# Seven block products instead of eight for the first f pair of a token pair's output, and two places for weights

## Chip, cores and metric

The kernel runs on one core of a Trainium2 chip. The metric is the device time in microseconds (us), the median of the runs; lower is better.

## What is computed

The reference is a channel attention and a mixture layer without routing behind it, over 4 batches of 6080 tokens with 256 channels and 2048 hidden features, all in float32:

```python
qn = q / (norm(q, axis=1) + 1e-06)          # q, k, v: (4, 6080, 256)
kn = k / (norm(k, axis=1) + 1e-06)
a = softmax(kn.transpose(0, 2, 1) @ qn / tau)   # (4, 256, 256)
x = (v @ a).reshape(24320, 256)
h = x @ w_in                                # w_in: (256, 2048)
g = where(h >= 1, h, where(h <= -1, 0, (h + 1) ** 2 / 4))
return g @ w_out                            # w_out: (2048, 256)
```

The attention's matrix is small, so the kernel multiplies it into w_in once per batch: the weights of a batch are a @ w_in, and h is v times these weights.

## The kernel before

**Precision.** A float32 value is held as two parts, a high one rounded for TensorE and a low one, the rest. `mm3` (L470 to L474) makes a product of two such values by three matmuls: high by high, high by low, low by high. Each matmul loads its 128x128 weights anew.

**Tiles and groups.** A batch has six token pairs: two tiles of 512 tokens each, of 480 in the last pair. The 2048 features are eight f pairs: two tiles of 128 features each. A group is one f pair of one token pair: 4 x 6 x 8 = 192 groups, f pairs innermost (`groups`). In one group h is a 2x2 block product (256 channels by 256 features, times two token tiles), and `strassen` (L640 to L656) makes it by 7 products of blocks: S1, S2, S3, S4 and A11, A12, A22 are sums or blocks of the weights, T1 to T4 and V11, V21, V22 those of v. Three PSUM banks carry them: A, B and one of two Z. In bank Z four of them run one after another, and between them ACT copies the bank (L644, L646) and DVE adds to it (L649, L653).

**The nonlinearity.** `tile_ops` (L782 to L799) makes g of each of the four h tiles of a group: ACT saturates (L790) and squares (L792), DVE takes the maximum with h (L794), ACT or DVE makes the high part (L796, L797), DVE the low part (L798). The pools are u (6 places of 512 columns) and g (7 places of two parts of 512).

**The output.** `o_ops` (L820 to L844) multiplies the four tiles by blocks of w_out, 8 products a group, two for each of the four output blocks (y, the token tile; ct, the channel tile). Each output block has a bank of its own, O00 to O11, in which it sums over the eight groups of a token pair; then ACT copies it (L838) and SP stores it to outT.

**Weights.** Each group needs 896 KB of weights in a place of pool w (w_mem, 4 places). In the first token pair of a batch they are computed or taken from what was computed (`make_W`, `take_W`; POOL makes the sums at L702, ACT the high parts at L706, DVE the low parts) and stored to w_d; in all others `load_W` reads them back from w_d.

**Work for the next batch** runs beside the groups: `gram_chunk` (k and q products), `square_piece` (squares of norms), `softmax` (which sends norms through HBM as rn_d and the matrix as e_d), `make_W7` (weights), and `make_V` for the next token pair (POOL subtractions at L746).

**What sets the order.** Every instruction is an `Op` with an engine, a modelled duration, what it reads and writes, and a due time; group g begins at due time 16 g. `Order.run` simulates the engines and hands out instructions one by one: on each engine the one that can start earliest, among those that can start now the one with the lowest due time. A place of a pool is free when all users of its last holder have been handed out, from the modelled end of the last of them. The program then runs in this order, each engine strictly in its own; SP issues every DMA.

Of the kernel before, what the change touches and what calls it, by code (L numbers as in the profile page):

```python
# [13 lines left out]
ALU = mybir.AluOpType  # L14
# [12 lines left out]
class Buf:  # L27


    def __init__(self, pool=None, ap=None):  # L30
        self.pool, self.ap = pool, ap
# [19 lines left out]
SOON = 0.3  # L51

# [6 lines left out]
class Order:  # L59
# [11 lines left out]
    def op(self, eng, dur, fn, r=(), w=(), due=0.0, gates=(), size=0, other=None, slack=0.0):  # L71
# [20 lines left out]
        o.bufs = list({id(b): b for b in (*r, *w)}.values())  # L92
# [32 lines left out]
    def run(self):  # L125
# [23 lines left out]
        while left:  # L149
            pick = None  # L150
            for e, ops in avail.items():
                now = free[e]
                best = None
                for o in ops:
                    t = base[o.n, e]
                    if best is not None and t > now + SOON and t >= best[0][0]:
                        continue
# [11 lines left out]
                    key = (now, o.due, o.n) if t <= now or o.due <= URGENT and t <= now + SOON else (t, o.due, o.n)  # L169
# [10 lines left out]
            for b in o.bufs:  # L180
                if b.ap is None:
# [4 lines left out]
                    b.ap = b.pool.aps[i]() if callable(b.pool.aps[i]) else b.pool.aps[i]  # L186
            for b in o.bufs:
# [38 lines left out]
U = 32  # L226
# [17 lines left out]
ET_SLACK = (2.0, 3.0)  # L244

# [10 lines left out]
def channel_attention_moe(ctx: ExitStack, tc: tile.TileContext, kq, kqT, vT, tau, w_in, w_out, outT):  # L256
# [42 lines left out]
    wout = sb("wout", [FP, 2, 2, C], F32R)  # L299

# [4 lines left out]
    def slot2(j, h):  # L305
# [3 lines left out]
        return late[j][:, h]  # L309

    w_mem = sb("w_mem", [4 * 2 * NS * P], F32R)
# [5 lines left out]
    u_mem = sb("u_mem", [6 * TB])  # L317
# [7 lines left out]
        "g": Pool([sb("g6", [2, TB], F32R), *[lambda j=j, h=h: slot2(j, h) for j in range(3) for h in range(2)]]),  # L325
        "w": Pool([w_mem[:, i * WSZ:(i + 1) * WSZ].rearrange("p (a j f) -> p a j f", a=2, j=NS) for i in range(4)]),
# [4 lines left out]
        "u": Pool([u_mem[:, i * TB:(i + 1) * TB] for i in range(6)]),  # L331
# [21 lines left out]
    pools["g"].held[1:] = [kq_all] * 6  # L353
# [10 lines left out]
    pools["u"].held[:4] = [u2_all] * 4  # L364
# [10 lines left out]
    def buf(pool):  # L375
        return Buf(pools[pool])
# [6 lines left out]
    def convert(src, out, dst, due, gates=(), step=0.4, load_due=None, n=1, keep=None):  # L383
# [6 lines left out]
        cb = buf("u" + two)  # L390
# [16 lines left out]
        if keep is not None:  # L407
# [4 lines left out]
           r=[cb, *out], w=out, due=due + 4 * step)  # L412

    wout_buf = [Buf(ap=wout[:, i]) for i in range(FP)]
    x_store = [Buf(ap=d) for d in x_dram]
# [5 lines left out]
    def make_w_out(i, due, gates=(), load_due=None):  # L421

        convert(w_out[i:i + 2].rearrange("n p a f -> p n (a f)"), wout_buf[i:i + 2],
                lambda x: wout[:, i:i + 2, x].rearrange("p n a f -> p n (a f)"), due, gates, load_due=load_due, n=2)
# [567 lines left out]
```

## Time and profile before

| | us |
|---|---|
| median of 3 runs | 2160.39 (2159.62 to 2161.54) |
| span of the profiled execution | 2158.3 |
| PE busy | 2147.2 |
| DVE busy | 1783.1 |
| ACT busy | 1593.0 |
| POOL busy | 245.0 |

The span is one execution's time from its first to its last instruction; the median is taken from whole runs and has some 2 us around it. Busy time is the time in which an engine works on something: PE is TensorE, DVE is VectorE, POOL is GpSimd, SP issues the DMAs. A busy time near the span tells which engine to look at first; whether it works without gaps, the waits and the stages tell.

### The profile page before, as it was taken

The numbers are of one execution on the slowest core, as the hardware profiler recorded it, in microseconds if no ns is written. First come the engines' busy times: TensorE is split into PE (matmuls) and PEld (weight loads), VectorE is DVE, ScalarE is ACT, GpSimd is POOL, SyncE is SP. The second block draws the span as 40 slices with busy tenths as digits, with TensorE's granted clock in tenths as the row PEclk, the third lists the DMA queues.
The fourth block names the chain that finished last, engine by engine and source line by source line (L and its number), as shares of the span: only waits on it lengthen the run. The fifth ranks groups of instructions, "written<-read, shape, count | busy, mean of one in ns | idle before, by whom it ended". The sixth has DMA issues, their size and how long they took to land.

```text
span 2158.3 us, 27952 instructions
## 1 busy us (share of the span) xinstructions
PE 2147.2 (99%) x9872; PEld 1802.1 (83%) x9872; DVE 1783.1 (83%) x2893; ACT 1593.0 (74%) x2818; POOL 245.0 (11%) x260
## 2 busy tenths in 40 slices
PE   9999999999999999999999999999999999999999
PEld 7888888888888888888888888888888888888887
DVE  7898888878798888888879888888787988777776
ACT  6687778777778777776778877777677777777776
POOL 0230020100131000000023000000012300001000
PEclk9999999999999999999999999999999999999999
DMA  9765366545665444544656455454556532332331
GB/s 385 299 225 172 130 205 206 174 164 156 202 222 181 172 158 163 202 156 133 198 174 234 173 183 172 154 192 140 138 201 202 173 124 91 132 126 94 121 120 36
DMA packets 124604, 371.46 MB, mean 172 GB/s; under 512 B 17968, under 2 KB 49584, under 8 KB 121904
## 3 DMA queue, kind: packets, MB, share of 16 engines
q1 hardware_dynamic: 124464, 369.67, 50.1%
q8 instruction: 78, 1.28, 0.2%
q14 instruction: 62, 0.51, 0.1%
HBM read 298.84 MB, written 70.78 MB: 171 GB/s over the span
## 4 chain that ended last, share of the span: by engine, by line
PE 96%; DMA 2%; DVE 1%; ACT 0%; POOL 0%; issue 0%; SPq 0%; ACTq 0%; DVEq 0%; POOLq 0%
PE bank L473 94%; PE bank L875 1%; DMA kq<-kq 1%; DMA raw_mem<-w_out 1%; DMA raw_mem<-vT 0%; DMA outT<-y_mem 0%; DVE mh_mem L891 0%; POOL t L746 0%; DVE u_mem L404 0%; ACT u_mem L790 0%; DVE w_mem L708 0%; ACT u_mem L792 0%; POOL cols L532 0%; DVE v L755 0%; DVE u_mem L401 0%
## 5 line engine op out<-in xcount | busy, mean ns | idle before, releaser
L473 PE MATMUL bank<-x,wout 128*128 128x512 f32 (+1 forms) x3948 | 1013.4, 388 | 0.0
L473 PEld LDWEIGHTS bank<-x,wout 128*128 128x128 f32 x3948 | 739.3, 188 | 147.0
L473 PE MATMUL bank<-v,w_mem 128*128 128x512 f32 (+1 forms) x3264 | 849.3, 388 | 1.1 <-ACT bank L646 0.6
L473 PEld LDWEIGHTS bank<-v,w_mem 128*128 128x128 f32 x3264 | 610.8, 188 | 122.9 <-ACT bank L646 1.2
L790 ACT ACTIVATE u_mem<-bank 128x512 f32<-128x512 f32 (+1 forms) x576 | 341.3, 593 | 252.9 <-PE bank L473 240.4
L794 DVE TENSOR_TENSOR u_mem<-bank,u_mem 128x512 f32<-128x512 f32 (+1 forms) x576 | 390.9, 680 | 131.3 <-ACT u_mem L792 130.2
L792 ACT ACTIVATE u_mem<-u_mem 128x512 f32<-128x512 f32 (+1 forms) x768 | 471.0, 626 | 6.8
L798 DVE TENSOR_TENSOR x<-u_mem,x 128x512 fp32r<-128x512 f32 (+1 forms) x658 | 457.1, 701 | 13.8 <-ACT x L796 8.7
L796 ACT CAST x<-u_mem 128x512 fp32r<-128x512 f32 (+1 forms) x300 | 183.9, 615 | 92.7 <-DVE u_mem L794 91.6
L649 DVE TENSOR_TENSOR bank<-bank,mh_mem 128x512 f32<-128x512 f32 (+1 forms) x198 | 137.2, 693 | 96.8 <-PE bank L473 93.0
L473 PE MATMUL bank<-x,w_mem 128*128 128x512 f32 (+1 forms) x768 | 208.8, 388 | 0.9 <-ACT bank L646 0.9
L473 PE MATMUL bank<-g,wout 128*128 128x512 f32 (+1 forms) x660 | 182.8, 387 | 0.0
L746 POOL TENSOR_TENSOR t<-raw_mem 128x512 f32<-128x512 f32 (+1 forms) x48 | 67.8, 1411 | 925.0 <-DMA raw_mem<-vT 542.7
L653 DVE TENSOR_TENSOR mh_mem<-bank,mh_mem 128x512 f32<-128x512 f32 (+1 forms) x198 | 135.6, 685 | 40.2 <-PE bank L473 35.2
L473 PEld LDWEIGHTS bank<-x,w_mem 128*128 128x128 f32 x768 | 143.6, 188 | 30.0 <-ACT bank L646 1.3
L797 DVE CAST x<-u_mem 128x512 fp32r<-128x512 f32 (+1 forms) x358 | 159.6, 452 | 8.0
L644 ACT COPY mh_mem<-bank 128x512 f32<-128x512 f32 (+1 forms) x198 | 115.3, 582 | 59.4 <-PE bank L473 57.3
L794 DVE TENSOR_TENSOR u_mem<-mh_mem,u_mem 128x512 f32<-128x512 f32 (+1 forms) x192 | 135.6, 706 | 13.6 <-ACT u_mem L792 13.3
L473 PEld LDWEIGHTS bank<-g,wout 128*128 128x128 f32 x660 | 123.7, 188 | 24.5
L646 ACT COPY bank<-bank 128x512 f32<-128x512 f32 (+1 forms) x198 | 113.4, 573 | 33.7 <-PE bank L473 28.0
L746 POOL TENSOR_TENSOR t<-raw_mem,t 128x512 f32<-128x512 f32 (+1 forms) x48 | 66.8, 1392 | 496.3 <-DVE v L755 394.1
L790 ACT ACTIVATE u_mem<-mh_mem 128x512 f32<-128x512 f32 (+1 forms) x192 | 118.9, 619 | 5.1 <-DVE mh_mem L653 3.7
(104 smaller groups left out, 1432.5 us busy)
## 6 DMA issues: line engine op xcount, KB each, us to landing
w_mem<-w_d SPq DMA_DIRECT2D x160, 896.0 KB, 4.6
raw_mem<-kqT SPq DMA_DIRECT2D x60, 512.0 KB, 6.2
w_d<-w_mem SPq DMA_DIRECT2D x32, 896.0 KB, 4.5
raw_mem<-kq SPq DMA_DIRECT2D x51, 512.0 KB, 5.5
kq<-kq SPq DMA_DIRECT2D x20, 1024.0 KB, 9.1
raw_mem<-vT SPq DMA_DIRECT2D x40, 512.0 KB, 6.3
outT<-y_mem SPq DMA_DIRECT2D x80, 256.0 KB, 2.8
win_mem<-wop_d SPq DMA_DIRECT2D x21, 512.0 KB, 5.6
```

The costliest lines, as they stand in the source:

```text
L473: nc.tensor.matmul(out, lhsT=lhs(a), rhs=rhs(c), start=start and m == 0, stop=stop and m == 2, skip_group_check=skip)
L644: op("ACT", act_us(n), lambda: nc.scalar.copy(m5.ap[:, :n], a.ap[:, :n]), r=[a], w=[m5], due=early)
L646: op("ACT", act_us(n), lambda: nc.scalar.copy(a.ap[:, :n], z.ap[:, :n]), r=[z], w=[a], due=early)
L649: op("DVE", dve_us(n), lambda: nc.vector.tensor_tensor(out=bb.ap[:, :n], in0=z.ap[:, :n], in1=m5.ap[:, :n], op=ALU.add), r=[z, m5], w=[bb] ...
L653: op("DVE", dve_us(n), lambda: nc.vector.tensor_tensor(out=h22.ap[:, :n], in0=z.ap[:, :n], in1=m5.ap[:, :n], op=ALU.add), r=[z, m5], w=[h2 ...
L746: op("POOL", pool_us(n), lambda: nc.gpsimd.tensor_tensor(out=tt(x), in0=a(), in1=c(), op=ALU.subtract), r=r, w=[ts[x]], due=due + d, gates ...
L790: op("ACT", act_us(n), lambda: nc.scalar.activation(us(), src(), IDENTITY_SAT240, scale=240.0), r=[h], w=[u], due=d_sat)
L792: op("ACT", act_us(n), lambda: nc.scalar.activation(us(), us(), AF.Square, bias=0.5, scale=1.0 / 480.0), w=[u], due=d_sq)
L794: op("DVE", dve_us(n), lambda: nc.vector.tensor_tensor(out=us(), in0=src(), in1=us(), op=ALU.max), r=[h], w=[u], due=d_max)
L796: op("ACT", act_us(n), lambda: nc.scalar.copy(t.ap[:, 0, :n], us()), r=[u], w=[t], due=d_hi, other=("DVE", dve1_us(n), lambda: nc.vector.t ...
L797: other=("DVE", dve1_us(n), lambda: nc.vector.tensor_copy(t.ap[:, 0, :n], us())) if g >= FIRST else None)
L798: op("DVE", dve_us(n), lambda: nc.vector.tensor_tensor(out=t.ap[:, 1, :n], in0=us(), in1=f32(t.ap[:, 0, :n]), op=ALU.subtract), r=[u], w=[ ...
```

## The change

The first f pair (i = 0) of every token pair but a batch's first (SPLIT) makes its output blocks by 7 products instead of 8. Four go straight to the four output banks (`direct`): two with blocks of w_out, two with sums of blocks (`wsum`, made once from w_out by DVE and ACT). Then the bank O01 goes on alone: ACT keeps a copy of it, a fifth product is added, DVE keeps the sum of it and a copy of O11, a sixth product is added, ACT keeps a copy, a seventh is added. The three kept tiles are added by DVE to the other three blocks when these are stored, in place of the ACT copy; O01 is then already whole. POOL makes the four differences of g tiles that the seven products need (`combos`), and three of these differences get high and low parts of their own.

To make room, pool w has two places instead of four. Pool u has 5 places of 1024 columns (one for two tiles), g has 4 places of two tiles; c and c2 hold the differences and the kept tiles. Due times are written out anew for groups of both kinds (T_PLAIN, T_STR; the numbers of T_PLAIN and most of T_STR are left out below), and a few others move. Operations on g tiles, in `tile_ops` before, are in `sat_ops`, `square_ops`, `max_ops` and `operand`, with the same instructions. The planner gets a branch for operations that start within AHEAD.

```diff
+AHEAD, RATE = -21.03, 40.8
...
-                    if best is not None and t > now + SOON and t >= best[0][0]:
+                    if best is not None and t > now + max(SOON, AHEAD) and t >= best[0][0]:
...
+                    if t <= now or o.due <= URGENT and t <= now + SOON:
+                        key = (now, o.due, o.n)
+                    elif t <= now + AHEAD and e in ("ACT", "DVE"):
+                        key = (now, o.due + RATE * (t - now), o.n)
+                    else:
+                        key = (t, o.due, o.n)
...
-U = 32
+U = 32.76
...
+SPLIT = ((0, 1, 1, 1, 1, 1), (0, 1, 1, 1, 1, 1), (0, 1, 1, 1, 1, 1), (0, 1, 1, 1, 1, 1))
+WN = 2
...
+T_STR = {
...
+    'sum': (30.04, 31.22, 27.0, 22.88),
+    'direct': (21.09, 27.49, 26.88, 27.74),
+    'chain': (30.85, 43.19, 53.35),
...
+    wsum = sb("wsum", [max(map(max, SPLIT)), 2, 4, P], F32R)
...
-    w_mem = sb("w_mem", [4 * 2 * NS * P], F32R)
+        return late[j] if h is None else late[j][:, h]
+
+    w_mem = sb("w_mem", [WN * 2 * NS * P], F32R)
...
-        "g": Pool([sb("g6", [2, TB], F32R), *[lambda j=j, h=h: slot2(j, h) for j in range(3) for h in range(2)]]),
-        "w": Pool([w_mem[:, i * WSZ:(i + 1) * WSZ].rearrange("p (a j f) -> p a j f", a=2, j=NS) for i in range(4)]),
+        "g": Pool([*[sb(f"g{i}", [2, 2, TB], F32R) for i in range(1)], *[lambda j=j: slot2(j) for j in range(3)]]),
+        "w": Pool([w_mem[:, i * WSZ:(i + 1) * WSZ].rearrange("p (a j f) -> p a j f", a=2, j=NS) for i in range(WN)], ordered=True),
...
-        "u": Pool([u_mem[:, i * TB:(i + 1) * TB] for i in range(6)]),
+        "u": Pool([u_mem[:, i * 1024:(i + 1) * 1024] for i in range(5)]),
+        "c": Pool([sb(f"c{i}", [TB]) for i in range(4)]),
+        "c2": Pool([sb(f"cc{i}", [2, TB]) for i in range(1)]),
...
+    def sum_w_out(k, part, cb, due):
+        t, o = buf("u", TB), wsum_buf[k]
+        tt = lambda m: t.ap[:, m * P:(m + 1) * P]
+        for m, a, c, o_ in ((0, lambda: part(0, 1), lambda: part(1, 1), ALU.add),
+                            (1, lambda: tt(0), lambda: part(0, 0), ALU.subtract),
+                            (2, lambda: part(0, 0), lambda: part(0, 1), ALU.subtract),
+                            (3, lambda: part(1, 0), lambda: tt(1), ALU.subtract)):
+            op("DVE", dve_us(P), lambda m=m, a=a, c=c, o_=o_: nc.vector.tensor_tensor(out=tt(m), in0=a(), in1=c(), op=o_),
+               r=[cb], w=[t], due=due)
+        flat = lambda a: wsum[:, k, a].rearrange("p m f -> p (m f)")
+        op("ACT", act_us(TB), lambda: nc.scalar.copy(flat(0), t.ap), r=[t], w=[o], due=due + 1)
+        op("DVE", dve_us(TB), lambda: nc.vector.tensor_tensor(out=flat(1), in0=t.ap, in1=f32(flat(0)), op=ALU.subtract),
+           r=[t], w=[o], due=due + 2)
...
+        u0, u1 = gu[g] = pair(), pair()
+        q = T_STR if i < SPLIT[b][k] else T_PLAIN
...
+        if i < SPLIT[b][k]:
+            combos(g)
+        at = lambda k: [(x, d + e) for x, e in q[k]]
+        gt[g, 1] = operand(u1, n, (at("hi1"), at("lo1")))
+        gt[g, 0] = operand(u0, n, (at("hi0"), at("lo0")))
...
+    def combos(g):
+        b, k, i = groups[g]
...
+        c2, c = sums[b, k, i] = buf("c2"), buf("c")
+        c2.parts, c.parts = [Buf(ap=()), Buf(ap=())], [Buf(ap=())]
+        for k_, out, o, a, x, c_, y in ((0, c2, 1, u1, 1, u1, 0), (1, u1, 0, u1, 0, u0, 0), (2, c2, 0, u1, 1, u1, 0),
+                                        (3, c, 0, u0, 1, c2, 0)):
+            op("POOL", pool_us(n), lambda out=out, o=o, a=a, x=x, c_=c_, y=y: nc.gpsimd.tensor_tensor(
+                out=half_of(out, o, n), in0=half_of(a, x, n), in1=half_of(c_, y, n), op=ALU.subtract),
+               r=[a.parts[x], c_.parts[y]], w=[out.parts[o]], h=[out, a, c_], due=d + T_STR["sum"][k_])
...
+    def strassen_o(g):
...
+        w_ = lambda j, x, ct: (lambda a: wout[:, j, a, x, ct * P:(ct + 1) * P])
+        s_ = lambda j, m: (lambda a: wsum[:, j, a, m])
...
+        first = T_STR["direct"]
+        mm(o(0, 1), w_(i, 0, 0), wout_buf[i], gt[g, 0], 0, i == 0, d + first[0])
+        mm(o(1, 0), s_(i, 3), wsum_buf[i], gt[g, 1], 1, i == 0, d + first[1])
+        mm(o(1, 1), s_(i, 0), wsum_buf[i], gt[g, 1], 0, i == 0, d + first[2])
+        mm(o(0, 0), w_(i, 1, 0), wout_buf[i], gt[g, 0], 1, i == 0, d + first[3])
+        if i < SPLIT[b][k] - 1:
+            return
+        r = sums[b, k] = {x: buf("c") for x in ((0, 0), "m5", (1, 0), (1, 1))}
+        early = d + T_STR["early"]
+        z = o(0, 1)
+
+        def copy(src, x):
+            op("ACT", act_us(n), lambda: nc.scalar.copy(r[x].ap[:, :n], src.ap[:, :n]), r=[src], w=[r[x]], due=early)
+
+        copy(z, (0, 0))
+        copy(o(1, 1), "m5")
+        late = lambda key, j: [(x, d + e + T_STR["late"] * (j - i)) for x, e in T_STR[key]]
+        t23 = [operand(sums[b, k, j][0], n, (late("hi2", j), late("lo2", j))) for j in range(SPLIT[b][k])]
+        for j in range(SPLIT[b][k]):
+            mm(z, s_(j, 1), wsum_buf[j], t23[j], 0, False, d + T_STR["chain"][0])
+        op("DVE", dve_us(n), lambda: nc.vector.tensor_tensor(out=r[1, 0].ap[:, :n], in0=z.ap[:, :n], in1=r["m5"].ap[:, :n],
+                                                            op=ALU.add), r=[z, r["m5"]], w=[r[1, 0]], due=early)
+        for j in range(SPLIT[b][k]):
+            mm(z, s_(j, 2), wsum_buf[j], t23[j], 1, False, d + T_STR["chain"][1])
+        copy(z, (1, 1))
+        for j in range(SPLIT[b][k]):
+            t = operand(sums[b, k, j][1], n, (late("hi4", j), late("lo4", j)))
+            mm(z, w_(j, 1, 1), wout_buf[j], t, 0, False, d + T_STR["chain"][2])
...
+                    r = sums.get((b, k), {}).get((y, ct))
+                    if r:
+                        op("DVE", dve_us(n), lambda o=o, yb=yb, r=r: nc.vector.tensor_tensor(
+                           out=yb.ap[:, :n], in0=o.ap[:, :n], in1=r.ap[:, :n], op=ALU.add), r=[o, r], w=[yb], due=due)
+                    else:
+                        op("ACT", act_us(n), lambda o=o, yb=yb: nc.scalar.copy(yb.ap[:, :n], o.ap[:, :n]), r=[o], w=[yb],
+                           due=due)
...
-            make_V(*groups[g + 4][:2], d + 8, gate(g), 7.0)
+            make_V(*groups[g + 4][:2], d + 8.3, gate(g), 5.42)
...
-                softmax(b + 1, d + 8)
+                softmax(b + 1, d + 19.26)
...
-    nc = bacc.Bacc("TRN2", target_bir_lowering=False, num_devices=1)
+    nc = bacc.Bacc("TRN2", target_bir_lowering=False, num_devices=1, dynamic_dma_scratch_size=1024)
```

## Rows read from the trace of the kernel before

**Rows 1.** The page: span; part 1, busy time by engine; part 4, the chain.

```profile
span 2158.3 us, 27952 instructions
...
PE 2147.2 (99%) x9872; PEld 1802.1 (83%) x9872; DVE 1783.1 (83%) x2893; ACT 1593.0 (74%) x2818; POOL 245.0 (11%) x260
...
PE 96%; DMA 2%; DVE 1%; ACT 0%; POOL 0%; issue 0%; SPq 0%; ACTq 0%; DVEq 0%; POOLq 0%
```

**Rows 2.** Waits of PE: waiter, released by: total us, times, longest us (first, last).

```profile
PE bank L875 <- DMA kq<-kq: 3.0, 4, 1.7
...
PE bank L473 <- DVE u_mem L794: 0.2, 1, 0.2
```

**Rows 3.** Stages: length, busy us (instructions) by engine, PE's clock, DMA share, GB/s.

```profile
100.00:150.00 50.00, 49.81 (x242) 41.86 (x241) 48.81 (x74) 40.07 (x74) 16.26 (x19) 1.00 0.60 211
1150.00:1250.00 100.00, 100.00 (x475) 84.01 (x474) 88.69 (x137) 79.08 (x138) 15.09 (x18) 1.00 0.58 202
1850.00:1950.00 100.00, 100.00 (x443) 82.84 (x442) 76.92 (x128) 71.16 (x127) 8.37 (x6) 1.00 0.36 123
```

**Rows 4.** Timeline of PE in batch 3: start, us, engine, line, operation, count.

```profile
1753.88 2.88 PE L473 MATMUL bank<-x,wout 128*128 128x512 f32 x12
1756.60 1.52 PE L473 MATMUL bank<-v,w_mem 128*128 128x512 f32 x6
```

**Rows 5.** Groups by line and form: busy us, mean ns | idle before, released by.

```profile
L798 DVE TENSOR_TENSOR x<-u_mem,x 128x512 fp32r<-128x512 f32 x549 | 385.2, 709 | 11.7 <-ACT x L796 7.6
...
L796 ACT CAST x<-u_mem 128x512 fp32r<-128x512 f32 x255 | 157.3, 619 | 69.7 <-DVE u_mem L794 68.5
...
L797 DVE CAST x<-u_mem 128x512 fp32r<-128x512 f32 x294 | 131.9, 455 | 6.4
...
L644 ACT COPY mh_mem<-bank 128x512 f32<-128x512 f32 x166 | 97.4, 587 | 54.9 <-PE bank L473 52.9
...
L746 POOL TENSOR_TENSOR t<-raw_mem,t 128x512 f32<-128x512 f32 x40 | 56.6, 1416 | 419.6 <-DVE v L755 334.7 <-DVE x L755 83.3
...
L838 ACT COPY y_mem<-bank 128x512 f32<-128x512 f32 x80 | 46.7, 583 | 14.2 <-PE bank L473 6.7 <-DMA outT<-y_mem 6.4
```

**Rows 6.** Timeline of PE in batch 3: S1, the last product before, next S1.

```profile
1781.76 0.84 PE L473 MATMUL bank<-v,w_mem 128*128 128x512 f32 x3
1782.44 0.84 PE L473 MATMUL bank<-x,w_mem 128*128 128x512 f32 x3
...
1791.96 0.84 PE L473 MATMUL bank<-v,w_mem 128*128 128x512 f32 x3
```

**Rows 7.** Timeline of ACT in batch 0, and at 1020 in batch 1.

```profile
119.87 0.59 ACT L644 COPY mh_mem<-bank 128x512 f32<-128x512 f32 x1 [0.67 <-PE bank L473]
...
121.92 0.94 ACT L706 CAST w_mem<-sf_mem 128x896 fp32r<-128x896 f32 x1
...
1020.79 0.59 ACT L644 COPY mh_mem<-bank 128x512 f32<-128x512 f32 x1 [0.40 <-PE bank L473]
```

**Rows 8.** Timeline of POOL, then of DVE, in batch 3.

```profile
1783.19 1.38 POOL L746 TENSOR_TENSOR t<-raw_mem,t 128x512 f32<-128x512 f32 x1
...
1783.79 1.33 DVE L794 TENSOR_TENSOR u_mem<-mh_mem,u_mem 128x512 f32<-128x512 f32 x1 [0.36 <-ACT u_mem L792]
...
1785.98 0.68 DVE L794 TENSOR_TENSOR u_mem<-bank,u_mem 128x512 f32<-128x512 f32 x1
```

**Rows 9.** DMA into w_mem: issues; SP's timeline; landing from 1010 and 1545.

```profile
w_mem<-w_d SPq DMA_DIRECT2D x160, 896.0 KB, 4.6
...
1019.81 0.37 SPq L556 DMA_DIRECT2D rn_d<-cols  x1
1021.47 0.32 SPq L379 DMA_DIRECT2D w_mem<-w_d  x1
...
DMA to landing us min/median/max: 13.5/13.5/13.5
...
DMA to landing us min/median/max: 12.6/12.6/12.6
```

More of the change, by code (lines that the diff above doesn't have):

```diff
@@ L69, in __init__, with op @@
         self.ops = []
-    def op(self, eng, dur, fn, r=(), w=(), due=0.0, gates=(), size=0, other=None, slack=0.0):
+    def op(self, eng, dur, fn, r=(), w=(), due=0.0, gates=(), size=0, other=None, slack=0.0, h=()):
         o = Op()
@@ new lines, in max_ops, with pair, operand @@
+    def max_ops(u, x, h, due, n):
+        us = lambda: half_of(u, x, n)
+        op("DVE", dve_us(n), lambda: nc.vector.tensor_tensor(out=us(), in0=h.ap[:, :n], in1=us(), op=ALU.max), r=[h],
+           w=[u.parts[x]], h=[u], due=due)
+    def pair():
+        u = buf("u")
+        u.parts = [Buf(ap=()), Buf(ap=())]
+        return u
+    def operand(u, n, dues, xs=(0, 1)):
+        t = buf("g")
+        t.parts = [Buf(ap=()), Buf(ap=())]
+        his, los = dues
+        part = lambda a, x: t.ap[:, a, :, :n] if x is None else t.ap[:, a, x, :n]
+        for x, due in his:
+            cols = n * (1 + (x is None))
+            op("ACT", act_us(cols), lambda x=x: nc.scalar.copy(part(0, x), part_of(u, x, n)), r=of(u.parts, x),
+               w=of(t.parts, x), h=[u, t], due=due,
+               other=("DVE", dve1_us(cols), lambda x=x: nc.vector.tensor_copy(part(0, x), part_of(u, x, n))))
+        for x, due in los:
+            op("DVE", dve_us(n * (1 + (x is None))), lambda x=x: nc.vector.tensor_tensor(
+                out=part(1, x), in0=part_of(u, x, n), in1=f32(part(0, x)), op=ALU.subtract), r=of(u.parts, x),
+               w=of(t.parts, x), h=[u, t], due=due)
+        return t
@@ new lines, in strassen_o, with mm @@
+    def strassen_o(g):
+        b, k, i = groups[g]
+        t0, n = pairs[k]
+        d = G * g
+        w_ = lambda j, x, ct: (lambda a: wout[:, j, a, x, ct * P:(ct + 1) * P])
+        s_ = lambda j, m: (lambda a: wsum[:, j, a, m])
+        if i == 0:
+            for y in range(2):
+                for ct in range(CT):
+                    o_buf[b, k, y, ct] = buf(f"O{y}{ct}")
+        o = lambda y, ct: o_buf[b, k, y, ct]
+        def mm(out, lhs, wb, t, x, start, due):
+            op("PE", mm_us(n), lambda: mm3(out.ap[:, :n], lhs, lambda c: t.ap[:, c, x, :n], start, True),
+               r=[t.parts[x], wb], w=[out], h=[t], due=due)
+        first = T_STR["direct"]
[24 more added lines that the diff above has]
+            mm(z, w_(j, 1, 1), wout_buf[j], t, 0, False, d + T_STR["chain"][2])
```

151 lines of the change are left out of this document (105 added, 46 removed).

## The prediction

> **What bounds the kernel now.** I read four views in this order: the page, the waits of TensorE, a table of stages, then the timeline of a few periods. The page says that PE is busy for 2147.2 us of the 2158.3 us span and that PE is 96% of the chain that ended last [rows 1]. A busy PE may still hide gaps, so the second view asks what PE waited for: six groups of waits, from 3.0 us down to 0.2 us, all but a few tenths of them in the start of the kernel [rows 2]. The table of stages then shows PE at 100.00 of 100 us in every batch, at a granted clock of 1.00 (the 2.4 GHz level), while DVE lies between 77 and 89 and ACT between 71 and 79 [rows 3]. So a matmul that goes away is time that goes away, as long as DVE, ACT, POOL and the loads of weights still arrive before PE asks for them. That second half is the whole question.
>
> **What a matmul is worth.** Busy time of one matmul (388 ns) overlaps the next, so I take distances between starts. Twelve 512-column matmuls run from 1753.88 to 1756.60: 0.2267 us each [rows 4]. For 480 columns I scale by 480/512: 0.2125 us.
>
> **The removed work.** Each product is three matmuls. A group (one f pair of one token pair) has 7 products for h and 8 for the output; the change makes 7 of the 8 in one group of each token pair except the first of a batch: 5 of 6 token pairs in 4 batches, 20 groups, 60 matmuls. Of each batch's five, four have 512 columns and one 480: 48 x 0.2267 + 12 x 0.2125 = 10.88 + 2.55 = **13.4 us** off PE.
>
> **The added work in such a group.** DVE: three more low parts, one sum of a bank and m5, and three of the four final copies, which become additions on DVE: seven instructions with two operands of 512 columns, 7 x 0.709 = 5.0 us by the low parts' row. Three more high parts go to DVE (0.455) or ACT (0.619): 1.4 us or 1.9 us. ACT: three copies out of banks (0.587) come, three final copies (0.583) go: nothing. POOL: four subtractions of 1.416 us: 5.7 us [rows 5]. All of it can lie beside PE if it fits. POOL is 11% busy [rows 1]. For DVE I compare with one token pair, 8 groups of 10.2 us (the distance of two S1 products, 1781.76 and 1791.96 [rows 6]), 81.6 us: in the fullest ordinary stage DVE is 88.69 busy in 100 us [rows 3], so 9.2 us are free; in the last batch 76.92, so 18.8 us are free. The demand of 5.0 to 6.4 us fits.
>
> POOL and DVE get in each other's way, and this speaks against the change. A DVE maximum of two SBUF operands took 1.33 us while a two-operand POOL subtraction ran (1783.19 to 1784.57); the same line with one operand in a bank took 0.68 at 1785.98, with POOL idle [rows 8]. If each of the four new POOL instructions stretches one DVE instruction by 0.65 us, DVE has 2.6 us more in such a group, 9.0 us in all: just under the 9.2 us that are free.
>
> The Trainium skill, GPSIMD Engine Reference, section Specifications, says that the SBUF interfaces of GpSimd are shared with VectorE and that instructions with two SBUF inputs contend. The trace agrees (1.33 against 0.68 us). By that rule 80 new POOL instructions give 80 x 0.65 = 52 us to DVE; were all of that passed on to PE, the sum would be 2160.4 - 13.4 + 52 = 2199 us, while by the row on PE's waits almost none of such stretching has reached PE.
>
> How much comes through to PE? The nearest row is PE's one wait for a maximum on DVE, 0.2 us, in the start, where DVE was 48.81 of 50 us busy [rows 2, 3]. It is a stage as crowded as a group of the new kind will be. From 0 to 0.2 us for each of 20 groups is 0 to 4 us; I take **2 us**.
>
> **The chain inside such a group.** The last three products run in one bank one after another, with an ACT copy, a DVE addition and an ACT copy between them. A copy takes 0.587 us [rows 5], its hand-over on top. While a copy runs PE has products of the following groups, as it has today for the four products of the h chain in bank Z. Cost 0 if the planner finds such products; the price if it doesn't is a rival.
>
> **Sums of w_out.** Four DVE subtractions of 128 columns, one ACT copy and one DVE subtraction of 512, once, in the start: no longer than six low parts of 0.709, so 0 to 4.3 us; only the part that PE would wait for counts and nothing needs the sums before group 8, so I take **1 us**.
>
> **Two places for weights instead of four.** Weights of group g+1 can be loaded when the last h product of group g-1 has read its weights. That product (A22 with T4) starts at 1782.44, right behind S1 of group g, and ends at 1783.28; S1 of group g+1 starts at 1791.96 [rows 6]. So a load has 8.7 us, where two more places gave two more periods, 29.1 us. The median of 160 loads lands in 4.6 us [rows 9]: 4 us to spare, cost 0. Queued behind such a load on SP are the raw loads of the next batch and the output stores; they wait a little more, and nobody is near needing them. In batch 0, where weights are computed, ACT writes the next ones 2.05 us behind its copy of S1's bank (119.87, then 121.92) [rows 7], when the last product of the group before, that comes right behind S1, is over: four places were hardly used there, cost 0.
>
> But one load in each of the first three batches takes far longer. At 1019.81 SP issues a store of 1 KB (the norms of the next batch, rn_d); the load of weights issued at 1021.47 behind it takes 13.5 us, and lands 15.2 us after the store's issue [rows 9]. Today that harms nobody. With two places a load issued x us behind the store comes 15.2 - x - 8.7 = 6.5 - x us late: nothing if it is issued ahead of the store or over 6.5 us behind it, at most 6.5 us, three times 0 to 19.5 us. Where does the store fall? It hangs on small DVE operations of softmax, whose due time moves from d+8 to d+19.26, that is by 11 of 16 parts of a period, some 7 us later if it decides at all. Today the store is issued about when S1 starts (ACT copies S1's bank at 1020.79, and S1 takes 0.84 us before that [rows 6, 7]); the load of weights would come some 1.5 us behind S1. A delay of the store by anything from 1.7 to 5 us puts it behind that load and far enough ahead of the next. I take **0**, with the range kept as a rival.
>
> **Due times and pools.** The new planner branch is idle: AHEAD is negative, so its condition never holds and the limit stays SOON. The new due times of ordinary groups, U and the spread of make_V reorder ACT and DVE work, without adding any: 0, within the 2 us taken above. SP gets no new DMA.
>
> **The sum.** Against the profiled execution: 2158.3 - 13.4 + 2 + 1 = 2147.9 us. The median of the runs is 2160.39, 2.1 us above that span, so **2150 us** (0.5% faster).
>
> **Rivals.**
> *Weights behind the store of norms.* If the store stays where it is, x is 1.66 as today, each batch loses 4.8 us, 14.5 us in all: 2164 us, no change. Half of it: 2157. For it: the loads behind the store took 13.5 us in batch 1 and 12.6 in batch 2 [rows 9], so the pattern repeats; against it: the moved due time.
> *Slower: groups of the new kind starve PE.* The new group needs four double places for operands at once, which is all that the pool has, its three late products hang on a chain POOL, ACT or DVE, PE, ACT or DVE, PE, and the stretched DVE work comes in one period: 9.0 us on top of a period in which DVE has 1.2 to 2.4 us free. If the products of the neighbours don't cover it, PE waits in each of 20 groups. It decides from 13.4 / 20 = 0.7 us a group; at 1.1 us a group the time is 2150 - 2 + 22 = 2170, slower. For it: DVE at 89 in the crowded stage; against: PE's waits of today, and five places of double size for h tiles, which let PE run ahead.
> *The saving doesn't come.* If spacing widens with the new operands, or the weights cost as much, within 4 us of today: 2160.
>
> **How the numbers follow.** What a measurement of this kernel can tell from no change is about 0.2%, 4.3 us: faster is below 2156.1, slower above 2164.7. Forecast, 2146 to 2154: 0.55. Better than that, with no new wait at all (2145): 0.05. Weights behind the store, 2154 to 2167: 0.22, of which 0.08 is still faster and 0.03 slower. Starved groups, 2154 to 2175: 0.13, of which 0.02 faster and 0.07 slower. No saving: 0.05. Faster 0.55 + 0.05 + 0.08 + 0.02 = 0.70, slower 0.10, same 0.20. The range of 8 in 10 takes the forecast's cases and most of the weights' bounds: 2146 to 2164.
>
> **What the profile after would show.** 9812 matmuls instead of 9872, still 0.2267 us apart. PE waits in the start only, if the forecast is right; a wait of PE for a DMA into w_mem, three times and right behind the store rn_d, for the first rival; waits of PE for ACT or DVE low and high parts, in every eighth group, for the second. DVE up by 100 to 180 us, POOL by 113 us. I am wrong if the chain that ended last holds more than 4 us of DMA in the middle of the span, or if PE's busy share of a late stage falls below 99.

## The result and the profile after

The changed kernel takes **2177.38 us** (median of 4 runs, 2175.71 to 2177.81) against 2160.01 for the kernel before (the three runs of the table above and one more): a ratio of 1.0076, interval 1.0062 to 1.009. It is slower by 17 us where 10 us less were forecast, and above the range of 2146 to 2164.

The page after, in the same parts as [rows 1]: span, busy time by engine, the chain that ended last.

```profile
span 2176.0 us, 28158 instructions
...
PE 2146.4 (99%) x9812; PEld 1786.8 (82%) x9812; DVE 1899.0 (87%) x3009; ACT 1649.3 (76%) x2914; POOL 365.6 (17%) x340
...
PE 85%; DVE 8%; DMA 2%; ACT 2%; issue 1%; POOL 0%; SPq 0%; ACTq 0%; DVEq 0%
```

The 60 matmuls are gone, but PE's busy time fell by 0.8 us only, and DVE has 8% of the chain where it had 1%. PE lost 2176.0 - 2158.3 + 13.4 = 31.1 us somewhere. Idle time (span less busy time) grew from 11.1 to 29.6 us, 18.5 of them; the other 12.6 us hide inside PE's busy time, because a run of matmuls that is held up between two of them is shown as one long busy stretch (as the three matmuls at 1858.96 below). PE's waits after, as in [rows 2] (waiter, released by: total us, times, longest us):

```profile
PE bank L555 <- DVE x L907: 5.7, 7, 1.1
PE bank L555 <- ACT bank L728: 5.4, 4, 1.4
PE bank L555 <- DVE bank L731: 5.4, 9, 1.1
...
PE bank L555 <- DMA w_mem<-w_d: 0.5, 1, 0.5
```

Most of this is new: before, PE's waits for DVE were 0.8 us in all and those for ACT 2.0, now they are 14.4 and 5.4. Low parts (L907) belong to ordinary tiles and to the new groups' differences alike; L728 and L731 are ACT's copy and DVE's addition in bank Z of the h products, which every group has. The wait for weights, the first rival, is 0.5 us. Two stages of [rows 3] after, a third from batch 3, and then three stretches of 10 us in batch 3, the last of which holds a new group's differences:

```profile
1150.00:1250.00 100.00, 99.12 (x469) 82.54 (x468) 92.62 (x136) 80.92 (x141) 20.71 (x24) 1.00 0.54 181
...
1750.00:1850.00 100.00, 98.90 (x437) 81.50 (x436) 83.32 (x138) 73.39 (x133) 12.72 (x9) 1.00 0.33 112
1850.00:1950.00 100.00, 99.59 (x435) 80.76 (x434) 88.97 (x143) 72.77 (x131) 18.03 (x12) 1.00 0.35 121
...
1830.00:1840.00 10.00, 10.00 (x46) 8.28 (x45) 9.17 (x17) 7.83 (x15) 1.30 (x1) 1.00 0.29 93
1840.00:1850.00 10.00, 10.00 (x46) 8.29 (x45) 8.47 (x16) 6.42 (x13) 0.00 (x0) 1.00 0.34 118
1850.00:1860.00 10.00, 9.95 (x44) 7.71 (x42) 9.96 (x14) 6.70 (x12) 6.42 (x4) 1.00 0.51 171
```

The clock is 1.00, so it isn't the clock. PE's busy share falls by about 1% at most in these stages; the count of matmuls shows the loss as well, 469 and 435 (first and third line) where [rows 3] has 475 and 443. In the last stretch DVE is full (9.96 of 10 us) and still ends only 14 instructions, where it ended 17 and 16 just before. This is what happens there (timeline: start, us, engine, line, operation):

```profile
1851.96 1.54 POOL L953 TENSOR_TENSOR cc<-u_mem 128x512 f32<-128x512 f32 x1 [16.83 <-DVE u_mem L888]
...
1853.97 0.68 DVE L1027 TENSOR_TENSOR y_mem<-bank,c 128x512 f32<-128x512 f32 x1
...
1854.57 1.18 DVE L907 TENSOR_TENSOR x<-u_mem,x 128x512 fp32r<-128x512 f32 x1
...
1857.00 1.62 POOL L953 TENSOR_TENSOR c<-u_mem,cc 128x512 f32<-128x512 f32 x1
...
1857.39 1.77 DVE L907 TENSOR_TENSOR g<-u_mem,g 128x512 fp32r<-128x512 f32 x1
...
1858.96 0.98 PE L555 MATMUL bank<-g,wsum 128*128 128x512 f32 x3
...
1861.89 0.68 DVE L907 TENSOR_TENSOR x<-u_mem,x 128x512 fp32r<-128x512 f32 x1
```

A low part (two operands in SBUF) takes 1.18 and 1.77 us beside POOL's subtractions and 0.68 behind them; an addition with one operand in a bank takes 0.68 beside POOL too. The three matmuls at 1858.96 need the stretched low part, and take 0.98 us where three take 0.84 [rows 6].

### The profile page after: what moved, and what is told of

Same layout as the page of the kernel before. It is cut to its first block, busy times and chain, and to the rows that moved or that the text cites. A ratio compares the mean times of both kernels' runs of the same rounds, so it can differ in the third digit from the quotient of the medians.

```text
span 2176.0 us, 28158 instructions
## 1 busy us (share of the span) xinstructions
PE 2146.4 (99%) x9812; PEld 1786.8 (82%) x9812; DVE 1899.0 (87%) x3009; ACT 1649.3 (76%) x2914; POOL 365.6 (17%) x340
## 4 chain that ended last, share of the span: by engine, by line
PE 85%; DVE 8%; DMA 2%; ACT 2%; issue 1%; POOL 0%; SPq 0%; ACTq 0%; DVEq 0%
PE bank L555 84%; DVE x L907 2%; DVE u_mem L888 1%; DMA raw_mem<-w_out 1%; PE bank L1067 1%; DVE g L907 1%; DVE x L905 1%; DVE y_mem L1027 1%; DMA kq<-kq 1%; DVE bank L731 1%; DMA raw_mem<-vT 1%; DVE mh_mem L735 0%; ACT L653 0%; ACT u_mem L879 0%; DVE kqs L565 0%
## 5 line engine op out<-in xcount | busy, mean ns | idle before, releaser
L555 PE MATMUL bank<-x,wout 128*128 128x512 f32 (+1 forms) x3225 | 821.9, 388 | 1.1 <-DVE x L907 1.1
L555 PEld LDWEIGHTS bank<-x,wout 128*128 128x128 f32 x3225 | 604.0, 188 | 122.2 <-DVE x L907 1.7
L879 ACT ACTIVATE u_mem<-bank 128x512 f32<-128x512 f32 (+1 forms) x576 | 341.4, 593 | 208.2 <-PE bank L555 201.0
L907 DVE TENSOR_TENSOR x<-u_mem,x 128x512 fp32r<-128x512 f32 (+1 forms) x574 | 418.8, 738 | 7.8 <-ACT x L903 3.7
L555 PE MATMUL bank<-g,wout 128*128 128x512 f32 (+1 forms) x1083 | 278.9, 388 | 0.7 <-DVE g L907 0.7
L903 ACT CAST x<-u_mem 128x512 fp32r<-128x512 f32 (+1 forms) x310 | 188.8, 614 | 71.0 <-DVE u_mem L888 66.8
L555 PEld LDWEIGHTS bank<-g,wout 128*128 128x128 f32 x1083 | 202.6, 188 | 42.0 <-DVE g L907 1.7
L731 DVE TENSOR_TENSOR bank<-bank,mh_mem 128x512 f32<-128x512 f32 (+1 forms) x198 | 136.9, 691 | 75.3 <-PE bank L555 73.8
L907 DVE TENSOR_TENSOR g<-u_mem,g 128x512 fp32r<-128x512 f32 (+1 forms) x194 | 145.6, 754 | 3.2 <-ACT g L903 1.7
L879 ACT ACTIVATE u_mem<-mh_mem 128x512 f32<-128x512 f32 (+1 forms) x192 | 119.4, 622 | 24.1 <-DVE mh_mem L735 23.4
L728 ACT COPY bank<-bank 128x512 f32<-128x512 f32 (+1 forms) x198 | 113.3, 572 | 29.7 <-PE bank L555 20.8
```

The lines of the kernel that those rows point to most:

```text
L555: nc.tensor.matmul(out, lhsT=lhs(a), rhs=rhs(c), start=start and m == 0, stop=stop and m == 2, skip_group_check=skip)
L728: op("ACT", act_us(n), lambda: nc.scalar.copy(a.ap[:, :n], z.ap[:, :n]), r=[z], w=[a], due=early)
L731: op("DVE", dve_us(n), lambda: nc.vector.tensor_tensor(out=bb.ap[:, :n], in0=z.ap[:, :n], in1=m5.ap[:, :n], op=ALU.add), r=[z, m5], w=[bb] ...
L879: op("ACT", act_us(n), lambda: nc.scalar.activation(half_of(u, x, n), h.ap[:, :n], IDENTITY_SAT240, scale=240.0), r=[h], w=[u.parts[x]], h ...
L903: op("ACT", act_us(cols), lambda x=x: nc.scalar.copy(part(0, x), part_of(u, x, n)), r=of(u.parts, x), w=of(t.parts, x), h=[u, t], due=due, ...
L907: op("DVE", dve_us(n * (1 + (x is None))), lambda x=x: nc.vector.tensor_tensor(out=part(1, x), in0=part_of(u, x, n), in1=f32(part(0, x)), ...
```

## The experiments

Each compares with the kernel before on the same chip (2160.3 to 2160.9 us throughout).

**Two places for weights alone.** The kernel before, with pool w of two places, taken in order:

```diff
-    w_mem = sb("w_mem", [4 * 2 * NS * P], F32R)
+    w_mem = sb("w_mem", [2 * 2 * NS * P], F32R)
-        "w": Pool([... for i in range(4)]),
+        "w": Pool([... for i in range(2)], ordered=True),
```

> The kernel before with two ordered places for weights in place of four, nothing else. If the places cost the time (theory places), the loss of the change against its own saving, 17 + 13 = 30 us, shows here: about 2175 to 2190 us. If the four POOL subtractions beside the low parts cost it (theory port), or the order of the new groups (theory plan), this stays near the kernel before: 2160 to 2166 us, with at most a few us behind the store of norms in three batches.

Measured: 2180.81 us, 1.0089 (1.0074 to 1.0104). PE's waits; the timeline of SP and, further down, of PE (start, us, engine, line, operation); then two stretches in the columns of the stages:

```profile
PE bank L473 <- DMA w_mem<-w_d: 7.9, 3, 3.1
```

```profile
1022.66 0.37 SPq L556 DMA_DIRECT2D rn_d<-cols  x1
1024.32 0.32 SPq L379 DMA_DIRECT2D w_mem<-w_d  x1
...
1036.24 1.99 PE L473 MATMUL bank<-v,w_mem 128*128 128x512 f32 x6 [3.11 <-DMA w_mem<-w_d]
1038.03 1.49 PE L473 MATMUL bank<-g,wout 128*128 128x512 f32 x3
```

```profile
1030.00:1036.00 6.00, 3.12 (x14) 2.26 (x12) 2.02 (x3) 2.60 (x5) 0.00 (x0) 1.00 0.59 139
1036.00:1040.00 4.00, 3.76 (x11) 3.06 (x12) 2.17 (x4) 2.16 (x4) 0.00 (x0) 0.66 0.22 38
```

The mechanism of the first rival exists: a load issued 1.66 us behind the store of norms comes late, once in each of three batches. Behind the wait three matmuls take 1.49 us instead of 0.84, and the granted clock from 1036 to 1040 is 0.66 in the mean: part of it at the 1.2 GHz level, after 6 us in which PE was busy for 3.12. Waits and clock together don't make 20 us; the rest lies in shorter gaps at the starts of batches and was not split further. The trace is of the fastest of four runs (2176.24 us, mean granted clock 0.999); the other three took 2180 to 2182 us at 0.997 to 0.998, so part of the 20 us isn't in it. Taken alone, this result lies in the range that was set for places as the cause. But in the changed kernel PE's wait for weights is 0.5 us, and the run with short differences below gives 22 us back with two places still in.

**Three places.** The same edit with 3 instead of 2.

> The kernel before with three ordered places for weights. Two places gave 2181 us, with PE waiting 7.9 us for three loads of weights behind the store of norms. With three, a load has 18.9 us instead of 8.7, more than the 13.5 us of the slowest. Theory store: the waits go, 2159 to 2163 us. If fewer places cost all along, by coarser order and not by three loads, about half of the loss stays: 2167 to 2173 us.

Measured: 2160.07 us, 1.0001 (0.9991 to 1.001). With a period more of lead the late load harms nobody. In the changed kernel the store is where the forecast put it, behind one load and 9.2 us ahead of the next (timeline of SP):

```profile
490.66 0.32 SPq L442 DMA_DIRECT2D w_mem<-w_d  x1
491.70 0.37 SPq L638 DMA_DIRECT2D rn_d<-cols  x1
500.86 0.32 SPq L442 DMA_DIRECT2D w_mem<-w_d  x1
...
518.82 5.32 SPq L684 DMA_DIRECT2D e_d<-u_mem  x8
524.24 0.40 SPq L442 DMA_DIRECT2D w_mem<-w_d  x1
```

What the forecast had not looked at is the lower pair: eight stores (e_d) take SP's queue for 5.32 us, their own waits included, and the load behind them is issued late. That is the wait of 0.5 us.

**No seven-product groups.** The changed kernel with `SPLIT` all zero: pools, due times, two places and tables stay.

```diff
-SPLIT = ((0, 1, 1, 1, 1, 1), (0, 1, 1, 1, 1, 1), (0, 1, 1, 1, 1, 1), (0, 1, 1, 1, 1, 1))
+SPLIT = ((0, 0, 0, 0, 0, 0), (0, 0, 0, 0, 0, 0), (0, 0, 0, 0, 0, 0), (0, 0, 0, 0, 0, 0))
```

> The changed kernel with SPLIT zero everywhere: pools, places, due times of ordinary groups and planner as changed, but every group makes eight products. Theory port and theory plan both expect the stalls to go with the new groups: 2158 to 2166 us. Theory places, or ordinary groups disturbed by the new due times, expect 2175 us or more, as 13.4 us of matmuls come back on top of the stalls.

Measured: 2170.88 us, 1.0046 (1.0029 to 1.0063). This lies in neither range. So the rest of the change costs 10.5 us by itself in that order; one of PE's waits is 3.0 us for weights, since in this order a load is issued 1.47 us behind the store of norms again (488.29, then 489.76).

**Short differences.** The changed kernel and its order; the four POOL subtractions work on 64 columns.

```diff
-                out=half_of(out, o, n), in0=half_of(a, x, n), in1=half_of(c_, y, n), op=ALU.subtract),
+                out=half_of(out, o, 64), in0=half_of(a, x, 64), in1=half_of(c_, y, 64), op=ALU.subtract),
```

> The changed kernel with the four POOL differences of a new group cut from 512 to 64 columns (the rest of the differences is left out), planned with the old length, so every engine has the same order; two buffers more are cleared at the start. Theory port, and a theory that the differences come late (latency), both expect PE's stalls in new groups to go: 2150 to 2156 us. Theory plan, by which the order itself leaves PE waiting, expects 2172 to 2178 us, as after.

Measured: 2155.43 us, 0.9975 (0.9965 to 0.9984): 22.0 us less than the changed kernel. But short subtractions are also done earlier, which the next one tells apart.

**Short differences, then POOL work that nobody waits for.** Behind the fourth short subtraction POOL subtracts constants five times, 1920 columns where 1792 were cut (POOL is busy for 410.7 us in all, where the changed kernel has 365.6):

```diff
+                if k_ == 3:
+                    for _ in range(5):
+                        nc.gpsimd.tensor_tensor(out=idle, in0=wide(ident), in1=wide(ones), op=ALU.subtract)
```

> As the run with short differences (the same part of the differences is left out), but behind the four short ones POOL makes five subtractions of 384 columns of constants into a tile that nobody reads: as many columns as were cut. Nobody waits for them. Theory port expects the stretched low parts on DVE and most of the stalls back: 2165 to 2178 us. If only the lateness of the differences counts (latency), it stays as with the short differences, 2150 to 2156 us.

Measured: 2178.11 us, 1.0081 (1.0066 to 1.0096): 22.7 us above e3, and back at the changed kernel, though its differences are early. The low parts of differences and POOL work, by line and form (busy us, mean ns | idle before): the changed kernel, then e3, then e4.

```profile
L953 POOL TENSOR_TENSOR cc<-u_mem 128x512 f32<-128x512 f32 x32 | 51.5, 1608 | 274.1 <-DVE u_mem L888 272.8
...
L907 DVE TENSOR_TENSOR x<-cc,x 128x512 fp32r<-128x512 f32 x24 | 24.7, 1028 | 0.1
```

```profile
L957 POOL TENSOR_TENSOR cc<-u_mem 128x64 f32<-128x64 f32 x40 | 20.9, 524 | 352.7 <-DVE u_mem L892 351.1
...
L911 DVE TENSOR_TENSOR x<-cc,x 128x512 fp32r<-128x512 f32 x24 | 16.4, 684 | 0.6 <-ACT x L907 0.5
```

```profile
L964 POOL TENSOR_TENSOR idle<-ident,ones 128x384 f32<-128x384 f32 x100 | 128.8, 1288 | 6.3
...
L913 DVE TENSOR_TENSOR x<-cc,x 128x512 fp32r<-128x512 f32 x24 | 25.3, 1055 | 0.1
```

And e3's busy times, from part 1 of its page:

```profile
PE 2137.2 (99%) x9812; PEld 1791.2 (83%) x9812; DVE 1852.2 (86%) x3009; ACT 1646.3 (76%) x2914; POOL 280.8 (13%) x345
```

The same 24 low parts take 1028, 684 and 1055 ns. So 22 us, 1.1 us for each of the 20 groups, are contention of POOL and DVE, and not differences that come late. PE's waits for DVE are 1.6 us in e3, where the changed kernel has 14.4. DVE's busy time is 1899.0 us with and 1852.2 with short subtractions: stretched by 46.8 us, of which PE paid 22.

**Exps together.** The timeline of the changed kernel at a softmax (at 515 us): ACT, then PE.

```profile
514.58 1.28 ACT L653 ACT_TABLE_LOAD   x1
515.88 0.51 ACT L653 ACTIVATE sf_mem<-sf_mem,cols 128x256 f32<-128x256 f32 x1
...
516.50 1.28 ACT L879 ACT_TABLE_LOAD   x1
517.79 0.57 ACT L879 ACTIVATE u_mem<-bank 128x480 f32<-128x480 f32 x1
518.38 1.28 ACT L653 ACT_TABLE_LOAD   x1
...
520.79 1.28 ACT L879 ACT_TABLE_LOAD   x1
...
526.55 0.92 PE L555 MATMUL bank<-v,w_mem 128*128 128x480 f32 x3 [1.40 <-ACT bank L728]
```

A saturation of ACT (L879) falls between the two Exps (L653). Each change of function loads a table for 1.28 us: four loads a batch where the kernel before has two. The edit issues both Exps at the place of the first, in the same plan:

```diff
-            op("ACT", ..., lambda it=it: nc.scalar.activation(
-                sv(it), sv(it), AF.Exp, ...),
+            op("ACT", ..., lambda it=it: [nc.scalar.activation(
+                sv(j), sv(j), AF.Exp, ...)
+                for j in ((it,) if b == 0 else (0, 1) if it == 0 else ())],
```

> The changed kernel, planned as it is, but the two exponentials of a softmax are issued one behind the other, where the first stood, in batches 1 to 3. After had two more loads of ACT's tables in each of three batches than before (1.28 us each), because a saturation lies between the two exponentials. Theory tables: PE's waits of some 2.8 us at each of the three places go, 2177 becomes about 2169 us. If these waits come from the places for weights or from the matrix store e_d, nothing changes: 2175 to 2179 us.

Measured: 2171.52 us, 1.0053 (1.0036 to 1.007): 5.9 us less than the changed kernel. PE's waits for ACT's bank copies fall from 5.4 to 1.2 us; those for weights rise from 0.5 to 2.9, so the loads by themselves may cost somewhat more than 5.9.

**Both: short differences and Exps together** (the edits of e3 and e5).

> Short differences (64 columns, the rest of the differences left out) and the exponentials together, order otherwise as in after. If the port and the tables are all that the change lost, this is the saving of 13.4 us bare: 2146 to 2149 us. If the two places for weights cost something of their own in the changed kernel, or the tables are not it, it stays at 2153 to 2157 us.

Measured: 2150.64 us, 0.9956 (0.9941 to 0.997), between the two ranges. The two causes nearly add up: each is worth about as much beside the other (20.9 us from e5, 4.8 from e3) as alone (22.0 and 5.9). What is left over 2160.3 - 13.4 = 2146.9 is 3.7 us; the largest new wait in it is for weights behind e_d's stores, which moved with the softmax (PE's waits, then the timeline of SP and PE):

```profile
PE bank L559 <- DMA w_mem<-w_d: 3.1, 3, 1.3
```

```profile
514.00 3.79 SPq L689 DMA_DIRECT2D e_d<-u_mem  x8
517.89 0.39 SPq L446 DMA_DIRECT2D w_mem<-w_d  x1
...
524.17 2.22 PE L559 MATMUL bank<-v,w_mem 128*128 128x480 f32 x9 [1.27 <-DMA w_mem<-w_d]
```

**No seven-product groups, Exps together** (the edits of e2 and e5).

> The changed kernel without any seven-product group (all pairs plain, SPLIT all 0) and, as in e5, both Exp activations of a softmax issued together: what is left of the change is two places for weights, the pools and the due times. Without the merging (e2) it took 2170.88 us, 10.5 above the kernel before. If the two causes found so far add up here as they did in e5 and e6 (4.8 to 5.9 us for the table loads), this gives 2165 to 2166 us, and the page still shows PE waits for a load of weights behind the store of norms (e2: one of 3.0 us). If the table loads harm only beside seven-product groups, it stays at 2171. If the table loads were all of the 10.5 us, it is 2160 to 2161.

Measured: 2168.13 us, 1.0034 (1.0024 to 1.0044): 2.8 us less than e2, not 5. Neither expectation holds in full. There was less to give back: in e2's order one of the three softmaxes has its Exps together already, so its trace has four table loads more than e8's, not six. And PE waits 4.6 us for weights in e8, where e2 waits 3.0. Some 3 us of its 7.5 are in no wait that I can name.

**An order that knows of the contention.** Nothing in the planner's model made DVE longer beside POOL. Here it is:

```diff
+            if o.eng == "DVE":
+                o.dur += min(o.two, 0.65 * max(0.0, pool_end - t))
+            if o.eng == "POOL":
+                pool_end = t + o.dur
```

> The changed kernel with all its seven-product groups, the exps together, and an order planned with the contention in it: a DVE instruction with two SBUF operands that starts while a planned POOL instruction runs is given up to 1.05 us more, a POOL subtraction 0.15 us more, the Exp pair its two table loads. Nothing is computed otherwise than in e5 (2171.52 us). If the 21 us are lost because the order doesn't know of the contention, and other work of DVE and PE could be put ahead, the time falls to 2151 to 2158 us and beats the kernel before. If they are lost because DVE has no room for the stretched work in those periods, or the order's own model gets in its way, it stays at 2168 to 2200 us (the plan itself is longer than that of the changed kernel, whose model is blind to it).

Measured: 2195.83 us, 1.0162 (1.0147 to 1.0177). Worse: PE waits 7.4 us for weights (the store of norms at 1032.04, a load at 1032.52 right behind it) and 5.1 us for DVE's additions into c. These due times, set for a model without the stretch, don't serve this one.

**The same with due times to match.** A milder stretch, for the differences alone, and new due times:

```diff
-                o.dur += min(o.two, 0.65 * max(0.0, pool_end - t))
+                o.dur += min(0.55 * (o.two > 0), 0.4 * max(0.0, pool_end - t))
-            if o.eng == "POOL":
+            if o.eng == "POOL" and o.two:
...
-    'max01': 36.97,   'sat11': 12.74,   'chain': (30.85, 43.19, 53.35),
+    'max01': ...,     'sat11': ...,     'chain': ...,      (68 numbers of T_PLAIN and T_STR; 60 in e11)
```

> e9 with two differences. The planner's stretch is milder and only for the differences: a DVE instruction with two SBUF operands that starts beside one of the four subtractions on POOL is given up to 0.55 us more, the subtraction 0.10 us more, the pair of Exps 2.4 us. And the due times within a group (the tables T_PLAIN and T_STR) are new: 37 numbers chosen by a random search for the shortest planned time under that model. Same computation as the changed kernel, both kinds of group, two places. The plan is 2139.1 us with 6.9 us of gaps on PE; for the kernel before the planner says 2154.0 with 8.4, and the chip took 2160.4. If the 21 us of the port are lost only because the order puts the stretched work where DVE is full, PE should have hardly any wait in seven-product groups, and the time is 2143 to 2153 us, faster than the kernel before and near the forecast of 2150. If there is no order in which DVE finds room, it stays at 2165 to 2175, whatever the plan says.

> As e10, with due times from another run of the same search, planned at 2142.2 us with 10.0 us of gaps on PE (3.1 us more than e10). If the plan with the contention in it tells what the chip does, this one comes 3 us behind e10, at 2146 to 2156 us; if the order can't help, both stay at 2165 to 2175.

Measured: e10 2160.06 us, 0.9999 (0.999 to 1.0009); e11 **2155.67 us, 0.9977 (0.9968 to 0.9987)**, faster than both kernels. e10 lies between its two ranges, e11 at the upper end of its first. That e11 would be 3 us behind e10 was wrong: e10's trace has one wait of 3.7 us for weights, where e11's has 0.5. Besides, e10's ten runs go from 2157.88 us, at a mean granted clock of 1.000, to 2162.43 at 0.998, while e11's ten are all at 1.000; the trace is of the fastest, so where the clock fell in the others isn't shown. e11's busy times, then the 12 us of a new group's differences in batch 3 and the 12 us before them (columns as in the stages):

```profile
PE 2139.0 (99%) x9812; PEld 1788.6 (83%) x9812; DVE 1872.9 (87%) x2947; ACT 1666.1 (77%) x2970; POOL 377.9 (18%) x340
```

```profile
1832.00:1844.00 12.00, 12.00 (x53) 9.50 (x52) 11.86 (x17) 8.88 (x17) 5.95 (x4) 1.00 0.52 179
1820.00:1832.00 12.00, 12.00 (x54) 9.95 (x53) 9.01 (x16) 8.27 (x16) 0.00 (x0) 1.00 0.24 85
```

DVE is as full beside POOL as it was (11.86 of 12 us), but PE is at 12.00 in that stretch, and DVE was 75% busy in the stretch ahead of it, where it was 88% in the changed kernel's two stretches above. That is one group. All 20, the 10 us from the first subtraction of each, summed, in e5 and then in e11 (both have the Exps together):

```profile
sum 200.00, PE 185.34 PEld 145.88 DVE 196.96 ACT 144.88 POOL 129.59; mean PE 9.27 PEld 7.29 DVE 9.85 ACT 7.24 POOL 6.48
```

```profile
sum 200.00, PE 197.89 PEld 163.14 DVE 196.05 ACT 152.40 POOL 130.23; mean PE 9.89 PEld 8.16 DVE 9.80 ACT 7.62 POOL 6.51
```

DVE is full in both, and PE is idle for 14.7 us in e5 and for 2.1 in e11. In the 20 us ahead DVE is 84% busy in e11 and 86% in the changed kernel over all groups, a smaller difference than in the one group. DVE has 62 instructions fewer than after, and ACT 62 more when the six table loads that went are counted: high parts that moved from DVE to ACT.

**e11 with short differences**, and **e11's due times with the planner as it was** (that is, e5 with those due times).

> e11 with its four subtractions on POOL cut from all columns to 64, planned at the old length (as e3 was made from the changed kernel; three quarters and more of the differences are left out of the computation). It measures how much of the port's cost is left in e11's order: the same cut was worth 22 us in the changed kernel. If e11's order keeps the stretched work away from POOL, little is left to gain: 2151 to 2156 us, 0 to 4 us below e11's 2155.67. If the order gained in other ways and the port still costs its 1.1 us a group, this falls by 15 to 22 us to 2134 to 2141.

> e5 (the changed kernel with the Exps together, planner blind to the contention, 2171.52 us) with only the due times of e11 put in. If the planner's knowledge of the contention is what helps, and the due times alone don't, this stays at 2165 to 2175 us. If the due times alone carry the gain, it is 2152 to 2160. The blind plan is 2147.3 us, 0.3 us longer than that of the changed kernel, so by its own model nothing is gained.

Measured: e12 2151.28 us, 0.9957 (0.9942 to 0.9971), 4.4 us below e11; e13 2169.41 us, 1.0038 (1.0025 to 1.005). e12's busy times (part 1 of the page):

```profile
PE 2136.3 (99%) x9812; PEld 1789.5 (83%) x9812; DVE 1829.9 (85%) x2947; ACT 1664.5 (77%) x2970; POOL 291.4 (14%) x345
```

In e11 the contention stretches DVE by 1872.9 - 1829.9 = 43.0 us, nearly the 46.8 of the changed kernel, and PE pays 4.4 us instead of 22. The order doesn't avoid the contention, but PE waits less for it; due times alone don't do that. How the order does it, by less DVE work ahead or by work of PE that is ready, was not told apart. Which part of e10's model mattered against e9's (the smaller stretch, the differences alone, the price of the Exps) was not told apart, nor was the kernel before searched in the same way, so how far it could fall is open.

## Why the prediction was wrong

**The saving of 13.4 us** stands. There are 9812 matmuls, and nine of 512 columns still follow one another in 2.04 us, 0.2267 each (starts at 1755.53 and 1757.57 in the changed kernel). With both causes taken away, e6 is 9.6 us below the kernel before.

**DVE's demand** was put too high, if anything: 6.4 us a group and 2.6 for the stretch. It measured (1852.2 - 1783.1) / 20 = 3.5 and 46.8 / 20 = 2.3 us. The 3.5 is a net figure: ACT made all of the 60 new high parts and 30 more (440 where it made 350; DVE 388 where it made 418), which took some 0.7 us a group off DVE.

**The step that failed** is "How much comes through to PE?": 0 to 0.2 us for each of 20 groups, 2 us taken. It measured 1.1 us a group, 22 us. Two things in it were wrong. The demand was held against the 9.2 us that DVE has free in eight groups, but it comes within one: four POOL subtractions lie within some 7 us, and there DVE is full (9.96 of 10). And the row chosen as nearest, one wait of 0.2 us in a crowded stage [rows 2, 3], was from an order planned without such a burst. The text saw both: the rival "groups of the new kind starve PE" says that the stretched work comes in one period in which DVE has 1.2 to 2.4 us free, and prices 1.1 us a group at 2170. That is the mechanism and the size that came, and it had a chance of 0.13. Its double places and its chain had no part that the runs show: with short differences (e3) PE waits 1.6 us for DVE in all.

The Trainium skill, GPSIMD Engine Reference, section Specifications, names the shared SBUF interfaces; the trace agrees (1028 against 684 ns). The sum made from it in the prediction, 52 us on DVE, is near the 46.8 measured; what neither the page nor the rows of before told is the share that reaches PE: 22 us in one order, 4.4 in another.

**Due times at 0** was the second failed step. They moved the softmax, which the text used to argue the store of norms away, and in the new order a saturation splits the Exps: six more table loads, 6 x 1.28 = 7.7 us of ACT, 4.8 to 5.9 us of time. Whether the softmax's own due time or those of the groups did it, no run tells apart. The rows of before show the loads' price in no group that I had taken, since in it nothing that needs the other table lies between the Exps. The Trainium skill, ScalarE: Activation LUTs, section Rules for kernel authors, says to group functions by table set and finish one set before the next; the trace agrees: e5 does that, and is 5.9 us faster.

**Two places at 0** held in its mechanism: PE's waits for weights are 0.5 us, since the store went behind the load as argued. The price kept for the rival (4.8 us a batch, 14.5 in all) was small against e1's 20 us in the kernel before. The e_d stores, which delay a load in the same queue, were missed, and are worth up to 3.1 us (e6).

**The rest**, chain and sums of w_out at 0 and 1 us, lies within the 3.7 us that e6 leaves, beside 3.1 us of waits for weights. Added up: 2160.3 - 13.4 + 21.5 (contention, between 20.9 and 22.0) + 5.4 (tables, between 4.8 and 5.9) + 3.7 = 2177.5, against 2177.4 measured. That it comes out is no test, since the 3.7 is what e6 leaves; the test is that each cause costs nearly the same with and without the other.

**The signs named** came, though only just. PE's busy share is 98.90 from 1750 to 1850, where at least 99 was asked of a late stage, but the other stages from 1650 on are above it. The chain that ended last holds 6.3 us of DMA in the middle of the span, where at most 4 were allowed (start, us):

```profile
524.24 6.30 DMA w_mem<-w_d
```

It is the load behind e_d's stores, for which PE waited 0.5 us, so this sign pointed at a small part of the loss; the waits for low parts and the count of matmuls in a stage showed the rest. DVE rose by 116 us and POOL by 121, as said. One reading was loose: of PE's 7.3 us of waits before, 0.9 lie between 170 and 250 us, where the text speaks of a few tenths outside the start; nothing rests on it.

## What to carry to other kernels

Work that is added to an engine beside the bound must be held against that engine's free time in the stretch where it falls, not against the mean of a stage; and where it contends with a neighbour, the stretch belongs in the model that makes the order, with due times set again for it: the same work cost 22 us in one order and 4.4 in the other. Before a due time is moved, look at what it will come to stand between (two Exps, a store and a load), since that is a price the moved step itself doesn't show.

## What the runs showed of the hardware that was not expected

- Beside a POOL subtraction of two SBUF operands, a DVE subtraction of two SBUF operands (128x512) took 1.03 us in the mean (the low parts of differences) and up to 1.77, against 0.68; POOL's own took 1.61 where the kernel before's two-operand subtraction took 1.42 [rows 5]. With one operand in a bank DVE's took 0.68 in either case.
- A change of table takes ACT 1.28 us each way (514.58 and 516.50 above), and the function behind it starts 0.01 to 0.02 us after its end.
- After one wait of 3.1 us (e1), PE's next matmuls ran for some microseconds at the 1.2 GHz level (three in 1.49 us; granted clock 0.50 from 1038 to 1040), where the stages of the changed kernel shown above, with their many short waits, are at 1.00.
